# Block-sorted attention and a maxout layer in one kernel: W2 turned by DMA in place of TensorE, with the first two items' work in another order

## The chip, the cores and the metric

One NeuronCore of a Trainium2 chip runs the whole program. The metric is the device time of one execution in microseconds (us); a version's time is the median of its runs. A profiled execution gives the page and the trace that are read here.

## The reference

```python
# attention: q, k, v are [4, 8, 768, 64], sort_net is [4, 8, 8, 8]
P = sort_net
for _ in range(5):
    P = P - max(P, axis=-1);  P = exp(P)
    P = P / (sum(P, axis=-1) + 1e-09)
    P = P / (sum(P, axis=-2) + 1e-09)
k_sorted = einsum('bhij,bhjcd->bhicd', P, k_blocks)      # 8 blocks of 96 rows
v_sorted = einsum('bhij,bhjcd->bhicd', P, v_blocks)
attn = softmax(scale * q_block @ k_sorted_block.T)       # inside a block only
x = attn @ v_sorted_block                                # to [3072, 512]
# maxout layer: w1, w2 are [512, 1024], w_out is [1024, 512]
out = maximum(x @ w1, x @ w2) @ w_out                    # [3072, 512], float32
```

## The kernel before, in words

The kernel works on four batch items of 768 tokens. It uses max(h1, h2) = relu(h1 - h2) + h2. So it forms W1 - W2 once (`w_difference`, L229), takes relu(x(W1 - W2)) as `g` (`moe_h`, L685), and puts the h2 part into one small matrix, wc = W2 Wout (`w_product`, L654). The output is then g Wout + x wc, twelve matmuls in two halves of six for each 128 tokens (`out_products`, L700).

W2 is needed turned for `w_product`. `w2_transposes` (L634) does that on TensorE: 16 transposes of 128x128 into a PSUM tile, copied to `w2T` by ACT or DVE. It is called twice, by the steps `tw0D` and `tw1A`.

For an item the steps are these. Loads go out on POOL's queue and cast float32 to bf16 on the way (`load_q`, `load_k`, `load_v`, `load_w`, `load_w_columns`, L132 to L189). `sort_k` (L449) and `sort_v` (L473, L493, L516) multiply with a block-diagonal form of P; for v, `turn_v` (L242) first copies the raw item into another order. `q_transposes` (L413) is TensorE work for items 0 and 1 and a DMA transpose on SP for items 2 and 3, after `pair_q` (L403) on DVE. `scores` (SC, L539) is eight small matmuls and one exp on ACT (about 0.8 us); `values` (VA, L567) is eight small matmuls, a reciprocal and a product on DVE. `x_transposes` (TR or tx, L600) turns x to `xT`: on TensorE for item 0, by a DMA on SP for the others. An x tile holds two VA, and a transpose waits for both. SC unit u has head pair u % 4 and token half u // 4; TR t has half t // 2 and reads VA 2t and 2t + 1.

All PSUM tiles share four buffers (L62). Copies out of PSUM go to ACT or DVE: named by the caller, or picked by `pick` (L96), which keeps a running load of both engines with fixed costs in ns. TensorE, ACT, DVE, POOL and SP each run their instructions in program order (`manual_schedule`, L64), so the order of the Python calls is each engine's order.

The start is hand-ordered. TensorE streams zero columns (`keep_streaming`, L77) while ACT and DVE do the five rounds on P (`sinkhorn`, L264); `p_bf` is P at the end. L762 to L777 issue POOL's work: W1 and W2 by column pieces, Wout, two of four W differences, and item 1's k. The list `front` (L783) then gives item 0's steps in order: `k`, `v`, `tq`, `SC`, `VA`, `tx`, `tw`, `diff`, `pe` (masks of later items) and `hCTa`, `hCTb` (token half C, column group T of `moe_h`, in two parts), with a last letter A or D for the copying engine; `F` adds a fill of 512 columns to the next step. Ahead of its last 26 steps stand the loads of q(1), v(1), v(2), k(2) (L830).

After that, item b's MoE work runs as units (L909): eight `moe_h`, then twelve halves of `moe_out`; for item 0, eight empty ones, four `w_product` (units 8 to 11) and twelve halves (12 to 23). After unit n come the steps that a table (`first_tail`, `second_tail`, `third_tail`) lists under n: the next item's attention. Two tiles make one output store of 512 KB on SP, after units 15, 19 and 23. `load_q(2)` reuses W2's buffer, `load_q(3)` and `load_k(3)` reuse `v_raw`.

Of the kernel before, what the change touches and what calls it, by code (L numbers as in the profile page):

```python
# [11 lines left out]
BF16 = mybir.dt.bfloat16  # L12
# [4 lines left out]
def kernel(  # L17
# [16 lines left out]
    nc = tc.nc  # L34
# [4 lines left out]
    B, H, S, D = q.shape  # L39
    NB = sort_net.shape[-1]  # L40
    BLK = S // NB
    G = B * H
# [109 lines left out]
    def load_k(b):  # L152
        k_raw[b] = (
            kpool.tile([128, HB * D], BF16, tag="k_raw", name="k_raw")
            if b < 3
            else v_raw[:, 0 : HB * D]
        )
        n = HB * D // NCH
        for ci in range(NCH):
            nc.gpsimd.dma_start(  # L160
                out=k_raw[b][:, ci * n : (ci + 1) * n],
                in_=k_src[b, :, ci * n : (ci + 1) * n],
            )

    def load_v(b, pieces=2, which=None, half=None):
        r0 = (b % 2 if half is None else half) * 64
        n = BLK * D // pieces
        for m in range(pieces) if which is None else [which]:
            nc.gpsimd.dma_start(
                out=v_raw[r0 : r0 + 64, m * n : (m + 1) * n],  # L170
                in_=v_src[b, :, m * n : (m + 1) * n],
            )
# [5 lines left out]
    def load_w(dst, src):  # L178
        s = src.rearrange("(t p) f -> p t f", p=128)
        n = s.shape[1] // 2  # L180
        for i in range(2):
            nc.gpsimd.dma_start(
                out=dst[:, i * n : (i + 1) * n, :], in_=s[:, i * n : (i + 1) * n, :]
            )

    def load_w_columns(dst, src, t0, t1):
        s = src.rearrange("(t p) f -> p t f", p=128)
        c = slice(t0 * DFF // 4, t1 * DFF // 4)
        nc.gpsimd.dma_start(out=dst[:, :, c], in_=s[:, :, c])  # L189
# [13 lines left out]
    def selections(b, eng=nc.gpsimd):  # L203
        heads = {0: (0, 1), 2: (2, 1), 3: (3, 3)}.get(b)
        if heads:
            sel_v[b] = const.tile([G, 2, 8, NB], BF16, tag=f"sel_v{b}", name="sel_v")
            for half, item in enumerate(heads):
                eng.tensor_copy(
                    out=sel_v[b][:, half],
                    in_=ident[0:G, item * 8 : item * 8 + 8].to_broadcast([G, 8, NB]),  # L210
                )
        if b == 0:
            return
        sel_k[b] = const.tile([G, 8, 16], BF16, tag=f"sel_k{b}", name="sel_k")
        eng.tensor_copy(
            out=sel_k[b], in_=ident[0:G, b * 8 : b * 8 + 8].to_broadcast([G, 8, 16])
        )
# [11 lines left out]
    def w_difference(t, eng=None):  # L229
        n = DFF // 4  # L230
        (eng or nc.vector).tensor_tensor(
            out=w1_sb[:, :, t * n : (t + 1) * n],
            in0=w1_sb[:, :, t * n : (t + 1) * n],
            in1=w2_sb[:, :, t * n : (t + 1) * n],
            op=ALU.subtract,
        )
        if not eng:
            load["D"] += 600
# [392 lines left out]
    w2T = big.tile([128, NFB, DMODEL], BF16, tag="w2T", name="w2T")  # L631
    wc = big.tile([128, HP, DMODEL], BF16, tag="wc", name="wc")

    def w2_transposes(t, eng):  # L634
        ps = ps_bf16("tw_ps")
        for n in range(16):
            fb, dmt = t * 4 + n // 4, n % 4
            nc.tensor.matmul(  # L638
                ps[:, n * 128 : (n + 1) * 128],
                w2_sb[:, dmt, fb * 128 : (fb + 1) * 128],  # L640
                ident,
                is_transpose=True,
                start=True,
                stop=True,
            )
        return lambda: evac(
            w2T[:, t * 4 : t * 4 + 4, :].rearrange("p f d -> p (f d)"),
            ps,
            2048,
            two_x=True,  # L650
            eng=eng,
        )

    def w_product(dmt):  # L654
# [95 lines left out]
        return SC, VA, TR  # L750

    first, second, both = slice(0, 64), slice(64, 128), slice(0, 128)
    keep_streaming(ps_f32("fill_ps"), 86 * 126, most=126)
    for it in range(5):
        sinkhorn(it)
        if it < 3:
# [5 lines left out]
    for c, n, m in [(2, 2, 0), (4, 3, 1)]:  # L762
# [1 line left out]
            out=maskJ[:, c : c + n],  # L764
            in_=maskJ[:, m].to_broadcast([128, NB, n]).transpose([0, 2, 1]),
        )
    for t in range(2):
        load_w_columns(w2_sb, moe_w2, t, t + 1)
        load_w_columns(w1_sb, moe_w1, t, t + 1)
    for b in range(1, B):  # L770
        selections(b)
    load_w_columns(w2_sb, moe_w2, 2, 4)
    load_w_columns(w1_sb, moe_w1, 2, 4)
    load_w(wo_sb, moe_w_out)
    w_difference(0, nc.gpsimd)
    w_difference(1, nc.gpsimd)
    load_k(1)  # L777
    turn_v(first, "A", 36, 56)
    turn_v(first, "A", 56, 80)
    block_diagonals_first()  # L780
    turn_v(first, "D", 80, 96)

    front = """  # L783
        k0D k1A k2D v1D v2A v3A tq0D v0A tq1D SC1 SC0 F1
        SC2 VA1 SC5 VA0 SC3 F2 VA2 SC4 F0 tx0D SC6 VA3
        SC7 h00a VA4 tx1A tw0D h01a VA5 h01bA diff2 h00bA VA7 tx2A
        tw1A h02a VA6 h02bA h11a diff3 tx3A h12a h03a h12bD h10a h10bA
        pe2 h11bD h03bA h13a h13bA
    """.split()
    fills = [0]  # L790

    def fills_due():
# [3 lines left out]
    def front_step(step):  # L796

        eng = step[-1] if step[-1] in "AD" else None
        name = step[:-1] if eng else step
        kind = name.rstrip("0123456789ab")  # L800
        n = [int(x) for x in name if x.isdigit()]
        if kind == "F":
            fills[0] = 512
        elif kind == "k":
            sort_k(0, n[0], 640 if step == front[0] else 0, eng)
        elif kind == "v":
            sort_v(0, n[0], 0, eng)
        elif kind == "tq":
            q_transposes(0, n[0], eng)
        elif kind == "SC":  # L810
            scores(0, n[0], fills_due())
        elif kind == "VA":
            values(0, n[0], fills_due())
        elif kind == "tx":
            x_transposes(0, n[0], eng)
        elif kind == "tw":
            w2_transposes(n[0], eng)()
        elif kind == "diff":
            w_difference(n[0])
        elif kind == "pe":  # L820
            block_diagonals([(0, 2), (0, 3), (1, 1), (1, 2), (1, 3)], 2)
        elif name[-1] == "a":
            moe_h_products(0, n[0], n[1], (0, 2), fills_due())
        else:
            moe_h(0, n[0], n[1], eng, (1, 3))

    for step in front[:-26]:
        front_step(step)

    load_q(1)  # L830
# [14 lines left out]
    def sorts_and_scores(b):  # L845
# [5 lines left out]
    TQ = [lambda half=half: q_transposes(1, half) for half in range(2)]  # L851
    TURN = [lambda c=c: turn(both, c) for c in (0, 24, 48, 72)]
    first_tail = {
        7: KS,
        9: [TQ[0], TURN[0]],
        10: [SC[0], TQ[1], TURN[1]],
        11: SC[1:4] + TURN[2:4] + [lambda half=half: load_v(3, half=half) for half in range(2)],
        12: VS[0:3],
        13: VS[3:6],
        14: VS[6:8] + [SC[4]],  # L860
        15: [VA[0], lambda: pair_q(2, 0)],
        16: [VA[1], lambda: pair_q(2, 1)],
        17: SC[5:8] + [TR[0]],
        18: [VA[2]],
        19: [VA[3], TR[1]],
        20: [VA[4]],
        21: [VA[5], TR[2]],
        22: [VA[6], VA[7], TR[3]],
    }
    SC, VA, TR, KS = sorts_and_scores(2)  # L870
    VS = [lambda t=t: sort_v_halved(3, t) for t in range(4)]
    TURN = [lambda c=c: turn(both, c) for c in (0, 24, 48, 72)]
    second_tail = {
        0: [lambda: q_transposes(2, 0), lambda: q_transposes(2, 1)],
        2: KS,
        4: SC[0:2],
        5: [VA[0]],
        6: SC[2:4] + [TURN[0]],
        7: [VA[1], TR[0]],
        8: [VA[2], TURN[1]],  # L880
        9: [VA[3], TR[1], TURN[2]],
        10: SC[4:7],
        11: [VA[4], TURN[3]],
        12: [VA[5], TR[2], lambda: load_k(3), lambda: load_q(3)],
        13: [VA[6]],
        14: SC[7:8] + VS[0:2],
        15: [VA[7], TR[3]],
        16: VS[2:4],
        17: [lambda: pair_q(3, 0)],
        18: [lambda: pair_q(3, 1)],  # L890
    }
    SC, VA, TR, KS = sorts_and_scores(3)
# [69 lines left out]
```

The softmax here doesn't subtract the row's maximum and nothing guards it: scores larger than these inputs give would overflow.

## Time and profile before

| | |
|---|---|
| median of 3 runs | 166.72 us (166.19 to 168.2) |
| profiled execution, its own time | 166.46 us |
| its span, first to last instruction | 164.7 us |
| TensorE matmul busy | 159.5 us |
| ACT, DVE, POOL busy | 83.1, 76.4, 32.7 us |
| granted TensorE clock, mean | 0.999 |
| loads on POOL's queue (q0) | 13.37 MB |
| stores and transposes on SP's queue (q1) | 10.17 MB |

PE is TensorE, PEld its weight loads, SP the engine that issues stores and transposes. The page divides the span into 40 slices of 4.1 us and gives each engine's busy share in tenths. The chain of work that ended last follows the end back from one wait to what released it; each row is a start, a duration and the work. Timelines list an engine's instructions with start, duration, line, tiles and, in brackets, the idle time ahead and what ended it. A window row gives each engine's busy time in a stretch, the granted clock, the share of the DMA engines, and GB/s.

### The profile page before, as it was taken

To read this page: it belongs to the slowest core of one execution; us is meant where nothing else is said; L and a number is where in the kernel's file an instruction comes from. 1 tells how busy PE (TensorE), PEld (TensorE's weight loads), DVE (VectorE), ACT (ScalarE), POOL (GpSimd) and SP (SyncE) were. 2 spreads that over 40 slices of the span, in tenths; PEclk is the share of its full clock that TensorE was granted. 3 is DMA by queue.
4 is the path that set the end of the run, shared out by engine and by line. 5 is a ranking of instruction groups with operands and counts; after the bars stand their busy time and mean duration, and the time that the engine had idled before them with its cause. 6 is when DMAs were issued, how large, how long until landed. Compare 5 with 4: busy or idle time off the path is not lost.

```text
span 164.7 us, 4563 instructions
## 1 busy us (share of the span) xinstructions
PE 159.5 (97%) x2018; PEld 96.6 (59%) x2018; DVE 76.4 (46%) x169; ACT 83.1 (50%) x102; POOL 32.7 (20%) x59
## 2 busy tenths in 40 slices
PE   7999899999999999999999999999999999999992
PEld 7958678756554555557655554575655546554451
DVE  5869778556375564535277863250642320000011
ACT  3585995918139846055652262557447206642020
POOL 7989687150104000000014010000000000000000
PEclk9999999999999999999999999999999999999999
DMA  3999999999999995688425999991025293000333
GB/s 51 200 204 197 199 208 205 210 204 220 207 205 211 218 232 108 175 116 210 98 31 97 186 193 227 184 229 12 0 52 175 50 179 128 0 0 0 127 131 128
DMA packets 30404, 23.90 MB, mean 145 GB/s; under 512 B 16752, under 2 KB 25200, under 8 KB 30384
## 3 DMA queue, kind: packets, MB, share of 16 engines
q0 software_dynamic: 11040, 13.37, 48.4%
q1 hardware_dynamic: 19200, 10.17, 26.2%
q8 instruction: 16, 0.26, 0.6%
q10 hardware_dynamic: 144, 0.07, 0.1%
q14 instruction: 4, 0.03, 0.1%
HBM read 26.75 MB, written 6.29 MB: 201 GB/s over the span
## 4 chain that ended last, share of the span: by engine, by line
PE 93%; DVE 3%; ACT 1%; issue 1%
PE out_ps L704 38%; PE h_ps L677 26%; PE fill_ps L82 6%; PE o_ps L575 5%; PE wc_ps L657 4%; PE s_ps L548 4%; PE k_ps L458 3%; PE tq_ps L433 2%; DVE kT L110 1%; PE v_ps L523 1%; PE tw_ps L638 1%; ACT e L556 1%; PE tx_ps L613 1%; PE v_ps L500 1%; DVE qT L110 1%
## 5 line engine op out<-in xcount | busy, mean ns | idle before, releaser
L704 PE MATMUL out_ps<-wo_sb,g 128*128 128x512 bf16 (+2 forms) x200 | 48.3, 371 | 0.1
L677 PE MATMUL h_ps<-xT,w_sb 128*128 128x384 bf16 x256 | 44.5, 326 | 0.0
L677 PEld LDWEIGHTS <-w_sb 128*128 128x128 bf16 x256 | 24.0, 98 | 15.6
L556 ACT ACTIVATE e<-s_ps 96x768 bf16<-96x768 f32 x32 | 23.9, 804 | 13.6 <-PE s_ps L548 13.3
L691 ACT ACTIVATE g<-h_ps 128x768 bf16<-128x768 f32 x27 | 21.8, 811 | 17.4 <-PE h_ps L677 17.3
L704 PEld LDWEIGHTS <-g 128*128 128x128 bf16 x200 | 17.1, 97 | 15.8
L704 PE MATMUL out_ps<-wc,xT 128*128 128x512 bf16 (+2 forms) x100 | 24.8, 370 | 0.0
L108 ACT COPY o<-out_ps 128x1024 f32<-128x1024 f32 x10 | 10.1, 1012 | 28.0 <-PE out_ps L704 25.2
L592 DVE TENSOR_TENSOR x<-o_ps,rs 96x512 bf16<-96x512 f32 x32 | 22.0, 687 | 1.1
L704 PEld LDWEIGHTS <-xT 128*128 128x128 bf16 x100 | 9.6, 97 | 11.2
L575 PEld LDWEIGHTS <-e 96*128 96x128 bf16 x256 | 11.8, 97 | 5.9 <-DVE v_sb L110 0.2
L586 DVE RECIPROCAL rs<-o_ps 96x8 f32<-96x8 f32 x32 | 6.4, 201 | 17.7 <-PE o_ps L575 17.5
L739 DVE COPY o<-out_ps 128x512 f32<-128x512 f32 (+1 forms) x2 | 1.2, 625 | 27.6 <-PE out_ps L704 27.6
L575 PE MATMUL o_ps<-v_sb,e 96*128 96x65 bf16 x256 | 12.9, 193 | 0.0
L110 DVE CAST kT<-k_ps 128x1024 bf16<-128x1024 f32 x7 | 8.3, 1215 | 9.4 <-PE k_ps L458 9.4
L108 ACT CAST v_sb<-v_ps 96x1024 bf16<-96x1024 f32 x10 | 9.8, 1013 | 2.5 <-PE v_ps L479 0.9
L693 DVE TENSOR_SCALAR g<-h_ps 128x768 bf16<-128x768 f32 x5 | 4.8, 956 | 10.8 <-PE h_ps L677 10.8
L110 DVE CAST v_sb<-v_ps 96x1024 bf16<-96x1024 f32 x6 | 7.3, 1217 | 5.1 <-PE v_ps L523 2.2
L160 POOL DMA_DIRECT2D v_raw<-in_k_dram x3 | 2.5, 839 | 35.2 <-DVE v_dc L250 31.4
L548 PEld LDWEIGHTS <-kT 64*128 64x128 bf16 x256 | 6.1, 94 | 5.5 <-issue 3.6
L548 PE MATMUL s_ps<-qT,kT 64*128 64x96 bf16 x256 | 8.6, 204 | 0.7 <-PE o_ps L575 0.4
L82 PE MATMUL fill_ps<-fill 128*128 128x126 bf16 x86 | 7.8, 280 | 1.2 <-DVE fill L73 1.2
(95 smaller groups left out, 143.5 us busy)
## 6 DMA issues: line engine op xcount, KB each, us to landing
out_dram<-o SPq DMA_DIRECT2D x11, 512.0 KB, 3.1
v_raw<-in_v_dram POOLq DMA_DIRECT2D x8, 384.0 KB, 12.7
k_raw<-in_k_dram POOLq DMA_DIRECT2D x9, 256.0 KB, 9.9
w_sb<-in_moe_w_dram POOLq DMA_DIRECT2D x4, 256.0 KB, 9.2
w_sb<-in_moe_w_dram POOLq DMA_DIRECT2D x2, 512.0 KB, 10.6
wo_sb<-in_moe_w_out_dram POOLq DMA_DIRECT2D x2, 512.0 KB, 14.4
v_raw<-in_v_dram POOLq DMA_DIRECT2D x3, 256.0 KB, 4.6
q_raw<-in_q_dram POOLq DMA_DIRECT2D x4, 192.0 KB, 8.8
```

Source lines behind the costliest of these rows:

```text
L82: nc.tensor.matmul(ps[:, 0:w], w0, fill[:, 0:w], start=True, stop=True)
L108: nc.scalar.copy(out=out_ap, in_=in_ap)
L110: nc.vector.tensor_copy(out=out_ap, in_=in_ap)
L548: nc.tensor.matmul(ps[:, h2 * 512 + ii * 128 : h2 * 512 + ii * 128 + BLK], kT[b][rows, (hp * 8 + i) * BLK : (hp * 8 + i) * BLK + 128], rhs ...
L556: nc.scalar.activation(out=e[:, 0 : 8 * BLK].rearrange("p (t c r) -> p t c r", t=8, r=R), in_=ps[0:BLK] .rearrange("p (t f) -> p t f", t=8 ...
L575: nc.tensor.matmul(ps[:, h2 * 512 + ii * 65 : h2 * 512 + (ii + 1) * 65], e[:, (h2 * 4 + ii) * BLK : (h2 * 4 + ii) * BLK + 128], v_sb[:, m0 ...
L586: nc.vector.reciprocal(out=rs, in_=ov[:, :, :, 64])
L592: nc.vector.tensor_tensor(out=x, in0=ov[:, :, :, 0:D], in1=rs.to_broadcast([BLK, 2, 4, D]), op=ALU.mult,)
L657: nc.tensor.matmul(ps[:, 0:512], w2T[:, fb, dmt * 128 : (dmt + 1) * 128], wo_sb[:, fb, :], start=(fb == 0), stop=(fb == NFB - 1),)
L677: nc.tensor.matmul(h_ps[ch, t][:, m * 512 : m * 512 + TCH], w1_sb[:, hp, fb * 128 : (fb + 1) * 128], xT[:, b % 2, ch, hp % 2, hp // 2, :], ...
L691: nc.scalar.activation(out=g, in_=src, func=AF.Relu)
L704: nc.tensor.matmul(dst, g_tiles[b, ch, m // 2][:, m % 2, off : off + 128] if m < NFB else xT[:, b % 2, ch, hp % 2, hp // 2, off : off + 12 ...
```

## The change

W2 is turned by four DMA transposes on SP, one for each 128 rows, and `tw` and its PSUM tiles go. The loads of W are issued in another order and at other places: W2's first piece after `p_bf`, the others after the first sorted k. This is done by small POOL copies into a new tile `seen`, each of which reads a few elements of what is to be waited for. A third copy reads `w2T` at the third transpose and stands ahead of the loads of q(1), v(1), v(2) and k(2). Item 0's list has another order, token half 1 first, and four fills in place of three, which now add up. The opening fill is 92 matmuls of 118 columns in place of 86 of 126. Item 1's attention moves from units 7 to 22 to units 11 to 23, `pair_q(2)` moves into the second table, and most of item 2's steps move by one or two units.

```diff
-    def w2_transposes(t, eng):
-        ps = ps_bf16("tw_ps")
-        for n in range(16):
-            fb, dmt = t * 4 + n // 4, n % 4
-            nc.tensor.matmul(
...
+    def w2_transposes(dmt):
+        nc.sync.dma_start_transpose(
+            out=w2T[:, :, dmt * 128 : (dmt + 1) * 128],
+            in_=w2_sb[:, dmt, :],
         )
...
-    keep_streaming(ps_f32("fill_ps"), 86 * 126, most=126)
+    keep_streaming(ps_f32("fill_ps"), 92 * 118, most=118)
...
-    for t in range(2):
-        load_w_columns(w2_sb, moe_w2, t, t + 1)
-        load_w_columns(w1_sb, moe_w1, t, t + 1)
-    for b in range(1, B):
-        selections(b)
-    load_w_columns(w2_sb, moe_w2, 2, 4)
-    load_w_columns(w1_sb, moe_w1, 2, 4)
-    load_w(wo_sb, moe_w_out)
-    w_difference(0, nc.gpsimd)
-    w_difference(1, nc.gpsimd)
-    load_k(1)
     turn_v(first, "A", 36, 56)
     turn_v(first, "A", 56, 80)
     block_diagonals_first()
+    seen = const.tile([128, 3, 2], BF16, tag="seen", name="seen")
+    nc.gpsimd.tensor_copy(out=seen[0:G, 0], in_=p_bf[:, NB - 1, NB - 2 :])
+    load_w_columns(w2_sb, moe_w2, 0, 1)
+    selections(1)
+    selections(2)
     turn_v(first, "D", 80, 96)
 
     front = """
-        k0D k1A k2D v1D v2A v3A tq0D v0A tq1D SC1 SC0 F1
-        SC2 VA1 SC5 VA0 SC3 F2 VA2 SC4 F0 tx0D SC6 VA3
-        SC7 h00a VA4 tx1A tw0D h01a VA5 h01bA diff2 h00bA VA7 tx2A
-        tw1A h02a VA6 h02bA h11a diff3 tx3A h12a h03a h12bD h10a h10bA
-        pe2 h11bD h03bA h13a h13bA
+        k1A k0A v1D k2A v2A v0D tq0D v3A tq1D SC4 SC5 F2
+        F3 VA4 SC6 SC7 VA5 F0 SC0 VA6 SC1 VA7 F1 SC3
+        tx2D SC2 tx3D VA1 h10a VA0 VA2 h10bA h11a tx0A h11bA diff3
+        VA3 diff2 h13a h01a tx1D h03a h13bD h03bD h01bA h12a pe2 h00a
+        h02a h00bD h02bA h12bA
     """.split()
...
-            fills[0] = 512
+            fills[0] += 512
...
-    for step in front[:-26]:
+    front_step(front[0])
+    c0 = int(front[0][1]) * 16
+    nc.gpsimd.tensor_copy(out=seen[:, 1], in_=kT[0][:, c0 : c0 + 2])
+    load_w_columns(w1_sb, moe_w1, 0, 1)
+    load_w_columns(w2_sb, moe_w2, 1, 2)
+    selections(3)
+    load_w_columns(w1_sb, moe_w1, 1, 2)
+    load_w_columns(w1_sb, moe_w1, 2, 4)
+    load_w_columns(w2_sb, moe_w2, 2, 4)
+    load_w(wo_sb, moe_w_out)
+    for dmt in range(HP):
+        w2_transposes(dmt)
+    w_difference(0, nc.gpsimd)
+    w_difference(1, nc.gpsimd)
+    load_k(1)
+    nc.gpsimd.tensor_copy(out=seen[:, 2], in_=w2T[:, NFB - 1, 382:384])
+    for step in front[1:-26]:
         front_step(step)
...
     first_tail = {
-        7: KS,
-        9: [TQ[0], TURN[0]],
-        10: [SC[0], TQ[1], TURN[1]],
-        11: SC[1:4] + TURN[2:4] + [lambda half=half: load_v(3, half=half) for half in range(2)],
-        12: VS[0:3],
-        13: VS[3:6],
-        14: VS[6:8] + [SC[4]],
-        15: [VA[0], lambda: pair_q(2, 0)],
-        16: [VA[1], lambda: pair_q(2, 1)],
-        17: SC[5:8] + [TR[0]],
-        18: [VA[2]],
-        19: [VA[3], TR[1]],
-        20: [VA[4]],
-        21: [VA[5], TR[2]],
-        22: [VA[6], VA[7], TR[3]],
+        11: KS,
+        12: [TQ[0]],
+        13: [SC[0], TQ[1]],
+        14: SC[1:4] + TURN[0:2],
+        15: SC[4:5] + TURN[2:4] + [lambda half=half: load_v(3, half=half) for half in range(2)],
+        16: SC[5:8],
+        17: VS[0:3],
+        18: VS[3:6],
+        19: VS[6:8],
+        20: [VA[0], VA[1]],
+        21: [VA[2], VA[3], TR[0], TR[1]],
+        22: [VA[4], VA[5], TR[2]],
+        23: [VA[6], VA[7], TR[3]],
     }
...
     second_tail = {
-        0: [lambda: q_transposes(2, 0), lambda: q_transposes(2, 1)],
+        0: [lambda: pair_q(2, 0), lambda: pair_q(2, 1)],
+        1: [lambda: q_transposes(2, 0), lambda: q_transposes(2, 1)],
         2: KS,
-        4: SC[0:2],
-        5: [VA[0]],
-        6: SC[2:4] + [TURN[0]],
-        7: [VA[1], TR[0]],
...
+        5: SC[0:2],
+        6: [VA[0], TURN[0]],
+        7: SC[2:4],
+        8: [VA[1], TR[0], TURN[1]],
...
```

More of the change, by code (lines that the diff above doesn't have):

```diff
@@ L632 @@
     wc = big.tile([128, HP, DMODEL], BF16, tag="wc", name="wc")
-    def w2_transposes(t, eng):
-        ps = ps_bf16("tw_ps")
-        for n in range(16):
-            fb, dmt = t * 4 + n // 4, n % 4
[L638 to L651, printed above, removed]
+    def w2_transposes(dmt):
+        nc.sync.dma_start_transpose(
+            out=w2T[:, :, dmt * 128 : (dmt + 1) * 128],
+            in_=w2_sb[:, dmt, :],
         )
@@ L815, in front_step @@
             x_transposes(0, n[0], eng)
-        elif kind == "tw":
-            w2_transposes(n[0], eng)()
         elif kind == "diff":
@@ L873 @@
     second_tail = {
-        0: [lambda: q_transposes(2, 0), lambda: q_transposes(2, 1)],
+        0: [lambda: pair_q(2, 0), lambda: pair_q(2, 1)],
+        1: [lambda: q_transposes(2, 0), lambda: q_transposes(2, 1)],
         2: KS,
-        4: SC[0:2],
-        5: [VA[0]],
-        6: SC[2:4] + [TURN[0]],
-        7: [VA[1], TR[0]],
-        8: [VA[2], TURN[1]],
-        9: [VA[3], TR[1], TURN[2]],
+        5: SC[0:2],
+        6: [VA[0], TURN[0]],
+        7: SC[2:4],
+        8: [VA[1], TR[0], TURN[1]],
+        9: [VA[2], TURN[2]],
         10: SC[4:7],
-        11: [VA[4], TURN[3]],
-        12: [VA[5], TR[2], lambda: load_k(3), lambda: load_q(3)],
-        13: [VA[6]],
+        11: [VA[3], TR[1], TURN[3]],
+        12: [VA[4], lambda: load_k(3), lambda: load_q(3)],
+        13: [VA[5], TR[2]],
         14: SC[7:8] + VS[0:2],
-        15: [VA[7], TR[3]],
+        15: [VA[6]],
         16: VS[2:4],
-        17: [lambda: pair_q(3, 0)],
+        17: [VA[7], TR[3], lambda: pair_q(3, 0)],
         18: [lambda: pair_q(3, 1)],
```

## The prediction

> **What bounds the kernel now.** I read the page first, then the chain of work that ended last, then one-microsecond windows, the timelines of POOL, DVE and SP, and last the DMA queues in short windows.
>
> ```profile
> span 164.7 us, 4563 instructions
> PE 159.5 (97%) x2018; PEld 96.6 (59%) x2018; DVE 76.4 (46%) x169; ACT 83.1 (50%) x102; POOL 32.7 (20%) x59
> DMA  3999999999999995688425999991025293000333
> ```
>
> TensorE works in all but 5 us, of which 1.2 lie ahead of its first matmul and 3 behind its last. DMA is full from slice 1 to 14 (4 to 62 us). So TensorE sets the end, and the loads are close behind it in the first 62 us.
>
> ```profile
> 24.97 0.89 PE tw_ps L638 x16
> ...
> 28.68 0.89 PE tw_ps L638 x16
> ...
> 35.61 2.71 PE h_ps L677 x16
> 38.31 1.64 PE k_ps L458 x96
> 39.95 3.56 PE wc_ps L657 x16
> ```
>
> In the chain the W2 transposes are on the path (1.78 us). The first item ends at 38.31, where the second item's `sort_k` follows; the product that reads `w2T` starts at 39.95.
>
> ```profile
> 18.00:19.00 1.00, 0.84 (x21) 0.56 (x18) 0.88 (x1) 0.94 (x2) 0.00 (x0) 1.00 1.40 187
> 19.00:20.00 1.00, 0.70 (x16) 0.49 (x15) 0.21 (x2) 1.00 (x3) 0.78 (x1) 1.00 1.47 196
> 20.00:21.00 1.00, 0.75 (x22) 0.62 (x24) 0.77 (x3) 0.96 (x2) 1.00 (x1) 1.00 1.32 202
> ```
>
> The second figure of a row is TensorE's busy time in that microsecond, the last one the GB/s moved. From 14 to 21 us TensorE is idle for 0.84 us in all; from 21 us to its last matmul it lacks 0.13. With the 1.78 this makes 2.6 us, and apart from fills (0.2 each) the change cannot win more.
>
> **What the Trainium skill says.** "DMA: Bandwidth & Descriptors", section "Queues, rings and completion order": each DMA engine goes round-robin between queues, a packet at a time. The DMA windows from 98 to 100 us, where `load_q(3)` meets an xT transpose, agree:
>
> ```profile
> q0 software_dynamic: 405, 0.31, 101.2%
> q1 hardware_dynamic: 272, 0.07, 27.5%
> ```
>
> In the next 2 us it is 354 to 462, so about one packet for one (0.25 KB for a transpose, 0.77 for q, about 1 for W, 2 for k, 6 for v). From 90 to 92 it is 672 against 59: not always so. The same page, section "Latency and other measured facts", gives 261 GB/s for a transpose whose middle dimension is strided, as `w2T`'s is. Here xT and qT, whole at the destination, show about 200 (0.79 MB of qT in 3.9 us). "TensorE: Matmul & The Clock Gate", section "Back-to-back issue gap", gives N/2.4 + 2.5 ns: 56 ns for 128 columns, and 0.89/16 is 56.
>
> **The change part by part.**
>
> *Opening fills.* 92 x 118 = 10856 columns in place of 86 x 126 = 10836; by that price cold (N/1.2) and warm agree within 0.05 us, and 12 fills of 512 and the wait for `p_bf` follow anyway: 0.
>
> *W2's transposes.* Two groups of 0.89 go: -1.78. Their evacuations (1.23 us DVE, 1.87 ACT) were beside matmuls and win nothing by themselves.
>
> *First item in another order.* I stepped the new list through with durations of the trace: e 0.77 apart, VA 0.24 on TensorE and 0.85 apart on DVE, half an h group 0.65, tx 0.34 and 0.54 or 0.80 to evacuate. Sorts and q transposes give the same evacuations to ACT and DVE, so the first e starts at 18.4 as now. DVE then sets the pace: VA4 to VA7 end at 23.05, tx2 at 23.6, tx3 at 24.3, and h10a starts at 24.05, which puts the end of the list at 36.15. Against 38.31 that is -2.15: the 1.78 and 0.35 of idle time (one fill of 0.22 more is in it). An error of 0.5 either way is likely.
>
> *W loads later.*
>
> ```profile
> 9.46 2.34 POOL L189 DMA_DIRECT2D w_sb<-in_moe_w_dram  x3
> ...
> 19.22 2.12 POOL L231 TENSOR_TENSOR w_sb<-w_sb 128x1024 bf16<-128x1024 bf16 x1 [1.56 <-DMA w_sb<-in_moe_w_dram]
> ...
> 25.64 0.92 POOL L143 DMA_DIRECT2D q_raw<-in_q_dram  x1
> ```
>
> POOL's queue is served in order of issue at about 205 GB/s: v, k and q of item 0 (2.36 MB) end at 15.9 by the summed windows, then each 0.26 MB piece of W takes 1.3 us. That gives 18.5 for the second piece, and w_difference(0) starts at 19.2. After: w2's piece 0 is issued at 11.3, behind `p_bf`; `w1`'s piece 0 at 14.2, behind the first kT (ACT, 13.9). Both are ahead of 15.9, so the queue never runs dry: 0. Three pieces, selections(3) and wo take POOL until 20.1; w_difference(0) then ends at 22.2 and (1) at 24.35; h10a wants the first at 24.05, h11a the second at 25.85. The last W2 piece lands at 26.9; DVE's diff3 waits for it, with VA3's rescaling behind, and ends at 27.6; h13a can start at 27.75. The cover here is 0.15 us: a microsecond of delay in W2 is a microsecond on the path.
>
> *Four DMA transposes.* SP has nothing else until 55 us. They start at 26.95, 1024 packets each, about 1.4 us of issue each (xT 1.22 for 768). At 28.1 the load queue still holds some 460 packets of wo and 384 of k. If served one for one, 844 of 4096 packets have gone when k ends at 35.3, and the rest follow alone. At 200 GB/s (0.83 MB, 4.2 us) the four land near 36, 37.4, 38.7 and 40. w_product wants them at 36.2, 38.0, 39.8 and 41.6: 0 to 0.2, taken as 0. If they win over the loads (the other ratio) all land by 34. k of item 1 slips from 35.7 to 36 to 38.7; its sort now comes at 43.5.
>
> *The gate on POOL.* Behind `seen[2]` stand load_q(1), four v pieces and load_k(2), then load_q(2). They are issued at 33 to 39 in place of 25.64, but before they were only queued: q(1) ended at 38.9. Now it lands at 43 to 45, and TQ0 wants it at 46.4. The v pieces (3.85 us for two) land by 48.5 and 52.7; TURN wants them at 50.6 and 52.3: 0 to 0.4 on DVE, taken as 0. v(3) ends at 65 to 68 in place of 61.3.
>
> *Second item later.* The same TensorE work is squeezed from 16 units into 12. Two waits appear. (a) VS6 and VS7 now come in unit 19, with its output evacuation ahead of them on DVE or ACT; VA0 one unit (1.30) later needs all of v_sb. VS7's copy ends about 1.85 after its matmuls, so 0.55 of wait; e5 to e7 on ACT hold up VS2's PSUM buffer by another 0.2 to 0.4, which I bound at 0 to 1.0 and take with (a) as 0.55. (b) TR1, now in unit 21:
>
> ```profile
> 69.52 0.20 DVE L586 RECIPROCAL rs<-o_ps 96x8 f32<-96x8 f32 x1 [0.62 <-PE o_ps L575]
> 69.76 0.69 DVE L592 TENSOR_TENSOR x<-o_ps,rs 96x512 bf16<-96x512 f32 x1
> 70.37 0.20 DVE L586 RECIPROCAL rs<-o_ps 96x8 f32<-96x8 f32 x1
> 70.59 0.69 DVE L592 TENSOR_TENSOR x<-o_ps,rs 96x512 bf16<-96x512 f32 x1
> ```
>
> These two VA started on TensorE at 69.08, and the second x is ready 2.2 later. TR1 then lands 2.8 to 3.7 later (8.3 under loads): 5.05 at least from the start of VA2. TensorE has 2 x 1.30 + 3 x 0.49 = 4.07 until item 1's h, and 0.33 to the matmul that reads TR1: a wait of 0.65 at least, 1.55 at 3.7, up to 3 if v(3)'s last packets share the engines. I take 0.65. TR3 stands behind a 512 KB store on SP, but its reader comes 7 us on: 0.
>
> *Second tail.* pair_q(2) moves behind h; its transposes (5.6) land ahead of SC in unit 5 (10.5 us on). The rest moves one or two units with slack: 0.
>
> Sum: -2.15 + 0.55 + 0.65 = -0.95, which makes a span of 163.75 against 164.7. Outside the span lie 1.8 us (166.46 - 164.7), untouched; on the median of 166.72 it gives 165.8.
>
> **Rivals.** (1) *Nothing is given back:* both waits vanish because ACT and DVE place their copies better than I stepped. 166.72 - 2.15 = 164.6. For it: before, the same VS copies made no gap. Against: TR1's 5.05 exceeds 4.4.
> (2) *The packed attention becomes the bound:* 1.0 for PSUM, 3 for TR1 under v(3), 0.4 for late v, 0.5 of the front's gain lost: 166.72 - 1.65 + 4.4 = 169.5; about half of it is 167.5. For it: an xT transpose took 8.3 us beside loads.
> (3) *Slower: the W2 transposes starve.* They keep less than their rate, by the strided destination or by loads. What remains at 35.3 is 0.83 MB, and the fourth is wanted at 41.6, so below 130 GB/s TensorE waits, and below about 115 the gain is gone. At 75 GB/s it lands at 46.4: +4.8, and 165.8 + 4.8 = 170.6. For it: an xT transpose under k loads ran at some 100 GB/s. Against: the gate keeps new loads out.
> (4) *It isn't what it says:* no, w_product reads only what the DMA wrote.
>
> **How the numbers follow.** Chances: forecast 0.50 (own range 164.9 to 166.8), rival 1 0.18, rival 2 0.20, rival 3 0.12. Two per cent, about what a measurement of this kernel can tell from no change, is 163.4 and 170.1. Below 163.4 exceeds the 2.6 us ceiling: 0.03, for scatter of the runs. Above 170.1: 0.10 of rival 3's 0.12 and 0.04 of rival 2's 0.20: 0.14. Within: 0.83. Range 164.0 to 169.3, which leaves out the worst of rival 3 and the tail of rival 2.
>
> **What would show it.** No tw_ps rows; the last h matmul of item 0 ends near 36 (over 37 refutes the stepping). wc_ps follows without a gap, or rival 3 holds. POOL's q_raw load starts between 33 and 39. Item 1's h has a gap of 0.6 to 1.6 at its third matmul. A wait of DVE or PE for a w_sb, q_raw or v_raw load ahead of 60 us would break the "0" of the load steps.

## The result and the profile after

The changed kernel takes 172.26 us (171.5 to 174.1) against 166.58 for the kernel before on the same chip: a ratio of 1.031, with an interval of 1.021 to 1.040. The forecast was 165.8 with a range of 164.0 to 169.3, so the change is slower where "about the same" was forecast. The profiled execution took 171.9 us. Of two runs below, e9 and e11, only the times and one figure of the clock are used, since e9's profiled execution ran at half clock from 21.4 to 28.3 us and e11's at 0.95 throughout.

First the page, the same three rows that were read of the kernel before:

```profile
span 169.8 us, 4501 instructions
PE 157.6 (93%) x1974; PEld 94.1 (55%) x1993; DVE 75.7 (45%) x169; ACT 80.4 (47%) x100; POOL 33.6 (20%) x62
DMA  3999999997999999999104999986025353000333
```

TensorE's matmuls sum to less (157.6 against 159.5 us; of the 1.9, a part is 19 matmul records that this trace lacks, x1974 beside x1993 weight loads) in a span that is 5.1 us longer: most of the loss is waiting. The DMA row used to be full to 62 us. Now (a digit is 4.2 us) it has a dent in its tenth digit, from 38 to 42 us, and is full again up to 80. The loads end later. The chain that ended last says where it hurts:

```profile
27.19 10.61 DMA w2T<-w_sb
...
44.93 1.64 PE k_ps L458 x96
...
67.73 6.55 DMA xT<-x
74.42 5.33 PE h_ps L663 x24
79.75 1.64 PE k_ps L458 x96
```

Two DMA transposes are now links of the chain, where the chain before had TensorE's `tw_ps`. The second `k_ps` row (the third item's sort) is a good mark, because the same work stands ahead of it in both kernels, `tw` and the fills aside. The chain before has

```profile
71.02 3.90 PE h_ps L677 x24
74.92 1.63 PE k_ps L458 x96
```

so the mark was at 74.92 and is now at 79.75, 4.83 later. From there to TensorE's end nothing more is lost (161.65 and 166.51: 4.86). So the whole answer lies ahead of 80 us. TensorE's timeline there, with the idle time and what ended it in brackets:

```profile
37.85 7.08 PE L643 MATMUL wc_ps<-wo_sb,w2T 128*128 128x512 bf16 x31 [1.23 <-DMA w2T<-w_sb]
...
65.48 0.66 PE L575 MATMUL o_ps<-v_sb,e 96*128 96x65 bf16 x16 [0.47 <-DVE v_sb L110]
...
74.42 5.33 PE L663 MATMUL h_ps<-xT,w_sb 128*128 128x384 bf16 x24 [2.91 <-DMA xT<-x]
```

Three waits, and one thing that is no wait: 24 h matmuls took 5.33 us, where the chain before has 3.90 for the same 24. The windows (second figure TensorE's busy time, then weight loads, DVE, ACT, POOL, the granted clock, DMA share, GB/s) show why:

```profile
72.00:73.00 1.00, 0.00 (x0) 0.00 (x0) 0.97 (x4) 0.06 (x1) 0.00 (x0) 1.00 1.58 144
73.00:74.00 1.00, 0.00 (x0) 0.00 (x0) 0.99 (x3) 0.00 (x0) 0.00 (x0) 0.81 0.98 198
...
76.00:77.00 1.00, 1.00 (x5) 0.50 (x4) 0.00 (x0) 0.00 (x0) 0.00 (x0) 0.50 1.00 268
```

While TensorE waited, its clock fell to half, and it stayed there until 77.0. The wait of 2.91 so cost another 1.43.

**Why the xT transpose was late.** POOL's timeline around the gate, and its last loads of v(3):

```profile
39.64 0.19 POOL L821 COPY seen<-w2T 128x2 bf16<-128x2 bf16 x1 [13.83 <-DMA w2T<-w_sb]
39.88 0.90 POOL L143 DMA_DIRECT2D q_raw<-in_q_dram  x1
...
53.99 0.53 POOL L169 DMA_DIRECT2D v_raw<-in_v_dram  x1 [5.52 <-DVE v_dc L250]
57.64 1.56 POOL L169 DMA_DIRECT2D v_raw<-in_v_dram  x3 [3.13 <-DVE v_dc L250]
```

POOL stood 13.8 us at the copy that reads `w2T`. All loads behind it, q(1) first, were issued from 39.88 on. The load queue (q0) had run dry before that, while SP's queue (q1) worked on: DMA windows (queue, packets, MB, share) from 37 to 38 us, then from 66 to 68 us:

```profile
q1 hardware_dynamic: 1009, 0.25, 128.5%
```

```profile
q0 software_dynamic: 83, 0.41, 100.3%
q1 hardware_dynamic: 7, 0.01, 2.1%
```

From 36 on the engines carried almost nothing but W2's transposes, and from 40 to 42 almost nothing (21 GB/s in each microsecond) until the first new load got going. That is some 6 us almost without loads at a time when they are the scarce thing: about four in which the transposes had the engines to themselves, and two in which nothing did. The debt shows at 66 to 68: v(3) still holds the engines in packets of 5 KB on average. The 7 packets of SP's queue are not transposes yet. They have 2 KB each and belong to an output store that was issued at 64.33, ahead of item 1's transposes, and that took until 73.5 to land. The first two transposes were issued at 67.73 and 69.52, their first packet of 256 bytes moved at 71.6, when v(3)'s packets were nearly over, and they landed 6.5 and 5.5 us after their issue.

### The profile page after: what moved, and what is told of

The parts are those of the page before. It is cut to its first block, busy times and chain, and to the rows that moved or that the text cites. A ratio compares the mean times of both kernels' runs of the same rounds, so it can differ in the third digit from the quotient of the medians.

```text
span 169.8 us, 4501 instructions
## 1 busy us (share of the span) xinstructions
PE 157.6 (93%) x1974; PEld 94.1 (55%) x1993; DVE 75.7 (45%) x169; ACT 80.4 (47%) x100; POOL 33.6 (20%) x62
## 4 chain that ended last, share of the span: by engine, by line
PE 68%; DMA 17%; DVE 5%; ACT 3%; issue 2%; POOL 2%; SPq 0%; ACTq 0%
PE out_ps L690 33%; PE h_ps L663 19%; DMA w2T<-w_sb 6%; DMA w_sb<-in_moe_w_dram 6%; PE wc_ps L643 4%; DMA xT<-x 4%; PE k_ps L458 3%; PE o_ps L575 3%; PE s_ps L548 3%; POOL w_sb L189 2%; ACT e L556 1%; DMA p_sb<-in_sort_net_dram 1%; PE v_ps L523 1%; PE tq_ps L433 1%; DVE colsum L276 1%
## 5 line engine op out<-in xcount | busy, mean ns | idle before, releaser
L663 PE MATMUL h_ps<-xT,w_sb 128*128 128x384 bf16 x256 | 45.4, 332 | 3.0 <-DMA xT<-x 2.9
L690 PE MATMUL out_ps<-wo_sb,g 128*128 128x512 bf16 (+2 forms) x185 | 45.8, 370 | 1.5 <-issue 1.1
L663 PEld LDWEIGHTS <-w_sb 128*128 128x128 bf16 x256 | 24.5, 99 | 19.5 <-DVE q_pair L407 3.0
L556 ACT ACTIVATE e<-s_ps 96x768 bf16<-96x768 f32 x32 | 23.8, 808 | 13.8 <-PE s_ps L548 13.6
L108 ACT COPY o<-out_ps 128x1024 f32<-128x1024 f32 x9 | 9.1, 1013 | 28.2 <-PE out_ps L690 25.6
L110 DVE CAST kT<-k_ps 128x1024 bf16<-128x1024 f32 x5 | 5.9, 1221 | 19.5 <-PE k_ps L458 19.5
L575 PEld LDWEIGHTS <-e 96*128 96x128 bf16 x256 | 10.9, 97 | 6.4 <-DVE v_sb L110 1.0
L575 PE MATMUL o_ps<-v_sb,e 96*128 96x65 bf16 x256 | 12.3, 193 | 0.9 <-DVE v_sb L110 0.5
L110 DVE CAST v_sb<-v_ps 96x1024 bf16<-96x1024 f32 x7 | 8.5, 1219 | 5.5 <-PE v_ps L523 2.6
L108 ACT CAST v_sb<-v_ps 96x1024 bf16<-96x1024 f32 x9 | 8.9, 1008 | 2.2 <-PE v_ps L500 0.9
L643 PE MATMUL wc_ps<-wo_sb,w2T 128*128 128x512 bf16 x31 | 7.0, 379 | 1.3 <-DMA w2T<-w_sb 1.2
```

The lines of the kernel that those rows point to most:

```text
L556: nc.scalar.activation(out=e[:, 0 : 8 * BLK].rearrange("p (t c r) -> p t c r", t=8, r=R), in_=ps[0:BLK] .rearrange("p (t f) -> p t f", t=8 ...
L575: nc.tensor.matmul(ps[:, h2 * 512 + ii * 65 : h2 * 512 + (ii + 1) * 65], e[:, (h2 * 4 + ii) * BLK : (h2 * 4 + ii) * BLK + 128], v_sb[:, m0 ...
L643: nc.tensor.matmul(ps[:, 0:512], w2T[:, fb, dmt * 128 : (dmt + 1) * 128], wo_sb[:, fb, :], start=(fb == 0), stop=(fb == NFB - 1),)
L663: nc.tensor.matmul(h_ps[ch, t][:, m * 512 : m * 512 + TCH], w1_sb[:, hp, fb * 128 : (fb + 1) * 128], xT[:, b % 2, ch, hp % 2, hp // 2, :], ...
L690: nc.tensor.matmul(dst, g_tiles[b, ch, m // 2][:, m % 2, off : off + 128] if m < NFB else xT[:, b % 2, ch, hp % 2, hp // 2, off : off + 12 ...
```

## The experiments

Theory A: the turning of W2 by DMA is the loss, through the order in which the DMA engines then serve things. Its transposes have to share with the loads, the gate then holds all later loads, so v(3) runs into item 1's transposes, and the clock falls behind that gap. Rival B: the packed second item (and the new order) are the loss in themselves, by ACT, DVE and PSUM. Rival C: the gate's wait is the loss, and without it all would be well.

| run | what differs | us | ratio to before (interval) |
|---|---|---|---|
| changed kernel | | 172.26 | 1.031 (1.021 to 1.040) |
| e1 | changed, no gate | 189.9 | 1.133 (1.128 to 1.138) |
| e2 | changed, TensorE turns W2 | 170.94 | 1.025 (1.020 to 1.030) |
| e3 | changed, half of v(3) | 169.78 | 1.019 (1.016 to 1.022) |
| e4 | changed, fills ahead of item 1's h | 171.58 | 1.028 (1.024 to 1.033) |
| e5 | before, new tables only | 169.1 | 1.015 (1.013 to 1.017) |
| e6 | changed, gate earlier | 173.16 | 1.033 (1.028 to 1.037) |
| e7 | changed, v(3) later | 175.26 | 1.054 (1.048 to 1.060) |
| e8 | e6 and e7 and spread VA | 176.61 | 1.063 (1.057 to 1.070) |
| e9 | before, new order only | 168.37 | 1.010 (1.008 to 1.012) |
| e10 | changed, old tables | 174.83 | 1.051 (1.046 to 1.055) |
| e11 | changed, nothing turned | 166.82 | 1.001 (0.999 to 1.003) |
| e12 | e9, nothing turned | 165.94 | 0.995 (0.993 to 0.997) |

**e1, no gate.**

```diff
-    nc.gpsimd.tensor_copy(out=seen[:, 2], in_=w2T[:, NFB - 1, 382:384])
```

> The changed kernel without the third POOL copy, so that the loads of q(1), v(1), v(2) and k(2) no longer wait for w2T. Theory A (the cost is the order in which the DMA engines serve loads and transposes): the w2T transposes now stand beside q and v packets too, so w2T lands after 43 instead of 37.8 to 40.7, the wait of TensorE at w_product grows from 1.65 us to over 5, the v(3) loads end earlier and the wait at item 1's first h shrinks; in all 171 to 176 us. Rival C (the 3 us in which the gate leaves the DMA engines idle are the loss): the time falls to 167 to 169. Rival B (the packing of item 1's attention into units 11 to 23): within 1 us of 172.3.

TensorE's timeline, and SP's with the four transposes in one row:

```profile
60.53 3.65 PE L643 MATMUL wc_ps<-wo_sb,w2T 128*128 128x512 bf16 x9 [17.61 <-DMA w2T<-w_sb]
```

```profile
28.50 31.12 SPq L635 DMA_TRANSPOSE w2T<-w_sb  x4
```

With the loads let through, the four transposes take 31 us and the product waits 3.08 and 17.61. So rival C falls: without the gate the loss is far larger. This is the forecast's third rival (the transposes starve), with more than four times the wait it was given there (4.8). The wait and the time were also far larger than Theory A had on record. The DMA windows, from 36 to 40 us and from 44 to 48, show how the two queues share:

```profile
q0 software_dynamic: 695, 0.56, 91.9%
q1 hardware_dynamic: 689, 0.17, 37.4%
```

```profile
q0 software_dynamic: 149, 0.72, 93.1%
q1 hardware_dynamic: 147, 0.04, 8.3%
```

It is one packet for one. But a transpose's packet has 256 bytes, and v's have 6 KB: beside them the transposes moved 0.04 MB in 4 us.

**e2, TensorE turns W2, all else as changed.**

```diff
-        VA3 diff2 h13a h01a tx1D h03a h13bD h03bD h01bA h12a pe2 h00a
+        VA3 diff2 h13a h01a tw0A tx1D h03a tw1A h13bD h03bD h01bA h12a pe2 h00a
...
-    for dmt in range(HP):
-        w2_transposes(dmt)
...
-    nc.gpsimd.tensor_copy(out=seen[:, 2], in_=w2T[:, NFB - 1, 382:384])
```

> The changed kernel with W2 turned on TensorE again (two groups of 16, after h01a and h03a), without the DMA transposes and without the gate on w2T; order of item 0, W loads and tails as changed. Theory A: no wait at w_product, v(3) ends near 63 us, ahead of TR0 and TR1, so that the wait at item 1's first h is 0.6 to 1.5 us and the clock stays up: 166.5 to 168.5. Rival B: the gap at item 1's first h stays near 2.9 us with the clock falling behind it: 170 or more.

The late xT transpose is gone as Theory A has it: the wait at item 1's h is 0.58 and the clock holds. The time missed the expectation by 2.4. TensorE's timeline shows where, around the place where `tw` was put back:

```profile
31.73 0.81 PE L677 MATMUL h_ps<-xT,w_sb 128*128 128x384 bf16 x4 [0.65 <-DVE xT L110]
32.69 1.05 PE L638 MATMUL tw_ps<-ident,w_sb 128*128 128x128 bf16 x16 [0.15 <-ACT w2T L108]
```

Item 0 ends at 39.95 there, 3.3 later than in the changed kernel: 1.78 is `tw`, the rest is mostly waits (the two shown, and one of 0.62 for a W difference, ending at 28.37). That the new order has no room for the two copies of `w2T` on ACT is likely, but only the wait of 0.15 names one. e2 is therefore no clean measure of "the change without its DMA transposes"; e11 was made for that.

**e3, half of v(3).**

```diff
-        15: SC[4:5] + TURN[2:4] + [lambda half=half: load_v(3, half=half) for half in range(2)],
+        15: SC[4:5] + TURN[2:4] + [lambda: load_v(3, half=1)],
```

> The changed kernel with v(3) loaded once, to one half of the partitions, instead of twice (left out: half of the reads for item 3's v, which then uses old data there), so that the loads end 3.9 us earlier. Theory A: TR0 and TR1 no longer stand behind 6 KB packets; the gap at item 1's first h falls from 2.9 to 0.6 to 1.5 us, the clock doesn't fall, 168 to 169.5. Rival B: no change of the gap, 171 to 172.5.

```profile
73.32 3.73 PE L663 MATMUL h_ps<-xT,w_sb 128*128 128x384 bf16 x22 [0.71 <-DMA xT<-x]
```

The gap at item 1's h goes from 2.91 to 0.71, the clock holds, and from the end of the product for wc to the mark it takes 31.35 us in place of 34.82. The time falls by some 2 us (ratio 1.019 in place of 1.031), a little less than expected (in this execution the product ended 0.8 later). So it is v(3)'s packets that hold up the output store and item 1's transposes behind it.

**e4, TensorE kept busy through the gap.**

```diff
-        units = [lambda ch=ch, t=t: moe_h(b, ch, t) for ch in range(2) for t in range(4)]
+        units = [
+            lambda ch=ch, t=t: moe_h(b, ch, t, n=6656 if (b, ch, t) == (1, 0, 0) else 0)
+            for ch in range(2)
+            for t in range(4)
+        ]
```

> The changed kernel with 13 fills of 512 columns (2.8 us of TensorE) ahead of item 1's first h, where TensorE waits. If the granted clock of 0.50 behind the gap costs the 1.43 us by which the 24 h matmuls are longer (5.33 against 3.90), the time falls by 1.2 to 1.5 us, to about 171, with the gap for xT still there. If the clock falls for another reason (a clock that changes by itself), the time stays within 0.5 us of 172.3 or grows by the fills.

```profile
75.76 3.74 PE L663 MATMUL h_ps<-xT,w_sb 128*128 128x384 bf16 x22 [0.22 <-DMA xT<-x]
```

22 h matmuls take 3.74 us here: full clock. From the product's end to the mark it takes 33.66, 1.16 less. The clock term is real in the trace; the two times' intervals overlap, so the total alone would not show it.

**e5, only the new tables, on the kernel before.** The two tables `first_tail` and `second_tail` are those of the changed kernel.

> The kernel before with only the two tables of the changed one (item 1's attention in units 11 to 23, pair_q(2) and item 2 later); W2 stays on TensorE, loads and item 0's order as before. Theory A with the packing as a smaller term: v(3) ends near 63 us, ahead of TR0, so only the packing is paid: 0.4 us of longer output groups behind small matmuls, 0.5 of wait for v_sb, 0.6 for TR1: 168 to 169. Rival B (the packing is the main loss): 170.5 or more, with a gap of over 2 us at item 1's first h. If the packing costs nothing: 166.2 to 167.2.

```profile
72.58 3.73 PE L677 MATMUL h_ps<-xT,w_sb 128*128 128x384 bf16 x22 [0.52 <-DMA xT<-x]
```

The mark moves from 74.92 to 76.32: 1.40, of which 0.47 is the wait for `v_sb`, 0.52 this one, and the remaining 0.4 is in output groups that stand behind small matmuls. (The time is 2.6 longer: TensorE ends 1.73 later than before, and what follows its last matmul takes 3.96 us in place of 3.05, which no run explains.) The gap at item 1's h is close to the forecast's 0.65, not 2.9. The reason is in the DMA window from 66 to 68 us:

```profile
q1 hardware_dynamic: 250, 0.47, 62.0%
q0 software_dynamic: 25, 0.10, 23.9%
```

v(3) was issued at 54.28, no earlier than in the changed kernel (53.99), but by 66 all but some 25 of its packets had moved here: it landed at 69.2, and at 73.1 there. From 62 to 64 us e5's load queue moves 0.35 MB in 72 packets (4.9 KB on average, v's), the changed kernel's 0.39 MB in 283 (1.4 KB, the last of q(2)'s and the first of v's): there k(2) and q(2) had stood in front of v(3) until then. Rival B is thus a real term of its own, but a smaller one; the larger gap needs the late loads.

**e6, the gate earlier.** The transposes and the gate go ahead of the loads of Wout and k(1).

```diff
-    load_w_columns(w1_sb, moe_w1, 2, 4)
     load_w_columns(w2_sb, moe_w2, 2, 4)
-    load_w(wo_sb, moe_w_out)
+    load_w_columns(w1_sb, moe_w1, 2, 4)
...
-    load_k(1)
     nc.gpsimd.tensor_copy(out=seen[:, 2], in_=w2T[:, NFB - 1, 382:384])
+    load_w(wo_sb, moe_w_out)
+    load_k(1)
```

> The changed kernel with the gate on w2T put ahead of the loads of W_out and k(1) (and w2's last piece loaded ahead of w1's). Theory A: behind W the load queue is empty, so the four transposes run alone from about 26.5 us and land by 31 (10.1 to 10.6 us of landing for the first two become 3 to 5); w_product then waits for W_out, which lands at 37 to 38, by 0.5 to 1.5 us; v(3) ends 2 to 3 us earlier than in the changed kernel and the gap at item 1's first h shrinks: 168.5 to 171. If transposes are slow by themselves (the strided destination), they land after 34 in spite of the empty queue and the time stays at 172 or more.

```profile
25.15 6.54 SPq L635 DMA_TRANSPOSE w2T<-w_sb  x4
```

```profile
41.40 8.95 PE L643 MATMUL wc_ps<-wo_sb,w2T 128*128 128x512 bf16 x28 [2.01 <-DMA wo_sb<-in_moe_w_out_dram]
```

Now the transposes run nearly alone (6.54 us of issue in place of 11.62) and the gate opens at 32.4. But Wout is late in their place: the product waits 1.42 and 2.01 for it, and after the second wait its matmuls take 0.32 on average in place of 0.22, the slow clock again. v(3) landed no earlier (73.6), and the time missed the expectation. The time that the turning takes from the loads (W's last piece landed at 27.4, the next load was issued at 32.7) is only handed to another load.

**e7, v(3) after item 2's q transposes**, by a POOL copy that reads `qT` ahead of `load_v(3)`; `TURN` of item 3 moves to units 11 to 13.

> The changed kernel with the loads of v(3) behind a POOL copy that reads qT of item 2, so that TR0 to TR3 of item 1 and the qT transposes have the DMA engines without loads; item 3's turns move to units 11 to 13 of the second table. Theory A: TR1 lands 2.8 to 3.7 us after its issue, the gap at item 1's first h is 0.6 to 0.8 us, the clock stays up: 168.3 to 169.8, if the late v(3) costs nothing further on. Rival B: the gap stays, 171 or more.

The gap at item 1's h is 0.50 and the mark is at 76.64, 3.1 better, as Theory A has it. But `qT` landed only at 82.8, so v(3) (issued 83.8 in place of 54), k(3) and q(3) all came late, and TensorE pays further on, once for `v_dc` (1.92) and once for the last item's k:

```profile
119.50 4.28 PE L663 MATMUL h_ps<-xT,w_sb 128*128 128x384 bf16 x16 [4.70 <-DVE kT L110]
```

**e8**, e6 and e7 together, with the values of item 1 spread over one unit more and the gate on the second transpose.

> Early gate (one transpose earlier), v(3) behind qT as in the run before, and item 1's values spread over units 19 to 23 with VA2, VA3, TR0 and TR1 in unit 20 and SC5 to SC7 in unit 19. Theory A: the waits at w_product (but for W_out, 0 to 1.5), at v_sb and at item 1's first h go; what is left of the change is the 1.7 us that item 0 gains, less 0.4 for output groups behind small matmuls: 164.8 to 167. If something further is behind the loss: 168 or more.

A miss. No wait is left at the product or at item 1's h, but TensorE waits 1.90 for a W difference, 1.68 and 1.92 for `v_dc`, and 1.91 for item 3's kT. Loads that are moved out of one place are missing at another (but the wait for a W difference is there in other runs too, up to 1.50 in e10).

**e10, the old tables in the changed kernel.**

> The changed kernel with the two tables of the kernel before (item 1's attention from unit 7 on). Theory A: q(1), issued behind the gate at 39.6 us, lands near 47 us, but its transposes now stand two units earlier, ahead of two of the four w_product groups, so that TensorE waits about 3 to 5 us for q(1) and again for v; TR0 and TR1 then stand behind v(3) too; 172 to 176. If the packing is what costs most: 169 to 170.5.

```profile
49.59 1.49 PE L433 MATMUL tq_ps<-ident,q_raw 128*64 128x128 bf16 x24 [6.35 <-DMA q_raw<-in_q_dram]
```

With the second item where it was, TensorE waits 6.35 for q(1), which the gate holds; the expectation had 3 to 5. So the later place of item 1's attention belongs to the gate: the turning by DMA needs it, and e5's 1.40 is part of the turning's price.

**e9, only item 0's order and the adding fills, on the kernel before** (`tw` stays on TensorE: `tw0A` behind `tx0A`, `tw1A` behind `diff2`).

> The kernel before with only item 0's list of the changed one (and its adding fills), W2 turned on TensorE after tx0 and after diff2; loads of W, tables and opening fill as before. The prediction gave the order itself 0.35 us of gain beside the 1.78 of the transposes: 166.0 to 166.4 by it. If the order gains nothing, or the two copies of w2T on ACT hold it up: 166.4 to 167.5. Above 168 the order would be a cause of the loss of its own.

**e11, the changed kernel with nothing turned; e12, e9 with nothing turned.** Both compute wc from other values:

```diff
-                w2T[:, fb, dmt * 128 : (dmt + 1) * 128],
+                w1_sb[:, dmt, fb * 128 : (fb + 1) * 128],
```

> The changed kernel, but W2 is not turned at all: the four DMA transposes and POOL's copy that waits for them are gone, and the product for wc reads the W difference in place of the turned W2, so that its values are others. All else stays: order of item 0, W loads, packed second item. It shows what the change is worth with the turning free. Theory A (the loss is what the transposes and their gate do to the loads and to item 1's transposes): item 0's h ends near 36.6 as in the changed kernel, no wait at the product, 0.5 to 0.7 at item 1's h, clock kept; of the changed kernel's 79.75 for the sort that follows item 1's h, 1.65 + 2.3 + 1.43 go: 74.4 to 75.2, and 166.5 to 168 us in all. Rival (the packing and the order are the loss): 169 to 171. The sum on record (front -2.15, packing +1.2) would give 165.8.

> The kernel before with item 0's new order and its adding fills, and W2 not turned at all (no TensorE transposes, no copies of them; the product for wc reads the W difference, so that its values are others). Loads, opening fills and second item are those of before. If the new order alone is worth the forecast's -2.15 once the 1.78 of TensorE transposes are gone: item 0's h ends near 36.2 and the time is 164.4 to 165. If the order costs by itself what the run with TensorE transposes and the new order suggested (1.6 us): 166.2 to 166.8.

e11 decides between A and B: with order, W loads and packed tables all kept, and only the four transposes and their gate gone, the time is that of the kernel before (1.001). The turning and its gate are worth some 5 us (1.031 against 1.001). All the rest together comes to nothing, although TensorE's 1.78 of transposes are gone in e11 too: the order, the W loads and the packing use them up. (The wait at the product, put at 1.65 in that expectation, is the 1.23 of the timeline above.)

e9 lost 1.7 where the forecast had a small gain for the order. e12, whose time lies between its two expectations, shows that TensorE's turning is dear in the new order (168.37 - 165.94 = 2.4 for 1.78 of matmuls; 3.3 in e2). Its chain of work that ended last, at the end of item 0:

```profile
33.64 3.36 PE h_ps L656 x20
36.99 1.64 PE k_ps L458 x96
```

Item 0 ends at 36.99 in place of 38.31. A gain of 1.32 with all of the 1.78 of `tw` gone means that the order itself costs about 0.5 with the old loads. And of the 1.32 little arrives: TensorE then waits 0.61 for the exp of a score at 50.4 and 0.61 for `qT` at 79.0, and item 2's h starts at 103.83 against 104.03. In time it is 0.8 (166.7 - 165.94). How the order's cost divides over its steps was not tried.

Of the versions that turn W2 none beats the kernel before.

## Why the prediction was wrong, point by point

The terms at the mark (third item's sort, 74.92 before and 79.75 after), each measured:

| term | forecast | measured | from |
|---|---|---|---|
| end of item 0 | -2.15 | -1.69 | 38.31 and 36.62 |
| wait for `w2T` | 0 | 1.23 | TensorE's timeline |
| packing, with 0.5 at item 1's h | 1.2 | 1.40 | e5's mark |
| more of the wait at item 1's h | 0 | 2.39 | 2.91 - 0.52 |
| half clock behind it | not foreseen | 1.43 | 5.33 - 3.90 |
| sum | -0.95 | 4.76 | 4.83 seen |

*Opening fills, evacuations, first item in another order.* Right in kind: it ended 0.47 later than stepped (36.15), within the error given. That is in part luck: with the same work up to there it ended at 37.04 in e3, 37.81 in e4, 37.67 in e7 and 38.05 in e10, beyond the 37 that was to refute the stepping. e12 says that what was won is `tw`, and that the 0.35 of idle time was not.

*W loads later.* 0 came out in this execution (TensorE waited 0.08 for diff3), and the warning that the cover is thin was right: the same loads and the same list have a wait of 0.27 at that place in e3, 0.65 in e7, 0.94 in e4 and 1.50 in e10.

*Four DMA transposes, "0 to 0.2, taken as 0".* Wrong in size, but not in its rule. The step took one packet for one while loads are queued. The Trainium skill, "DMA: Bandwidth & Descriptors", section "Queues, rings and completion order", says that engines go round-robin between queues, a packet at a time, and the trace's packets agree. From 32 to 34 us they are

```profile
q0 software_dynamic: 199, 0.36, 95.0%
q1 hardware_dynamic: 196, 0.05, 18.1%
```

and e1 has 695 to 689. What was wrong is the start. The step counted from 28.1; the first transpose was issued at 27.19, and no packet of it moved before 31.1, 3.9 us later. It is 3.9 to 4.0 in e1, e3, e4, e7 and e10 too, and 1.3 in e6 and e8, where the load queue was about to end. Why it is so long beside queued loads, no run shows. So at 35.3 some 420 packets had gone, not 844. What was left then ran alone at 252 GB/s in the window shown and 284 in the next, near the 261 that the same page gives in "Latency and other measured facts" and above the 200 taken. The four landed at 37.8, 38.7, 39.6 and 40.7 where 36, 37.4, 38.7 and 40 were stepped: the late start put the first 1.8 late, and the first is the one that the product waits for.

*The gate on POOL, "taken as 0".* This is the step that failed. The time of issue was forecast closely (33 to 39, seen 39.88), and q(1) was in time for TensorE, though 2 us later than given (46.95). But "before they were only queued" was taken to mean that holding them costs nothing. That holds while the queue in front stays full. Here it ran dry at 36.6, the next load packet moved at 41.5, and some 6 us of loading were lost. So v(1) and v(2) came late (DVE waited 2.07 for `v_raw`, which the forecast had named as a sign against it), k(2) and q(2) stood in front of v(3), and v(3) landed at 73.1, where 65 to 68 was given. At the mark this is 2.39 + 1.43 = 3.82 of the 5.8 us between forecast and measured; 1.23 is the wait for `w2T`. e11 takes the turning and its gate away together, so how the loss divides between the gate and the transposes' own time on the DMA engines stays open.

*TR1, 0.65, "up to 3 if v(3)'s last packets share the engines".* The small size is right (0.52 in e5). The condition for the large one was named and its price was right (2.91), but it was put into rival 2 with a chance of 0.20, though it followed from the gate's step. Two steps were costed one by one, each with the other at its best. The transpose that h waited for is also TR0 (74.28) and not TR1. A 512 KB store stands ahead of both on SP's queue, which the step had for TR3 alone; whether the gap closes when that store is issued behind them was not tried.

*The clock.* No step had it. The Trainium skill, "TensorE: Matmul & The Clock Gate", section "Part 1: The HAM clock gate (the "warmup" mystery)", says that TensorE falls to half clock after an idle window of about 3.4 us, and needs about as long busy to come back. Here the mean of 0.81 from 73 to 74 puts the fall at 73.6, 2.1 after the last matmul (71.5), and full clock returns at 77.0, 2.6 after work resumed. The half clock so lasted 3.41 us, as long as the page's window, but 2.1 of idle time was enough to bring it on; there the measurement decides. The other traces narrow it down. Ahead of the last matmul, half clock lasts 3.41 us in all of them (e7, and twice in e8) or a multiple of it (6.83 in e6 and e10, 17.07 in e1). Counted from its changes in such steps, the clock fell after a step with 1.90 or 1.92 us idle (e8), 2.12 (the changed kernel) or 2.19 (e6), or idle throughout (e1, e7, e10); it held after steps with 1.67 and 1.68 (e8) or 1.85 (e1). The edge is near 1.9 us and not sharp, as e9's execution at reduced clock fell after 1.81. So e8's wait of 1.90, inside one step, cost the clock, and e7's of 1.92 and e1's of 3.08, each across two, did not. The wait of 2.91 had to be priced with the clock at risk.

*Rivals.* Rival 2 (169.5) had the mechanism, and lacked the clock and the wait for `w2T`. Rival 3 (170.6) had the direction and is what e1 shows, but in the changed kernel the gate turned that loss into late loads. Its "against", that the gate keeps new loads out, was true and was the cost.

*Ceiling.* No run won more than the 2.6 us; e12 shows that with the turning free some 0.8 of it arrives.

## What to carry to other kernels

A gate that holds loads back is free only as long as the DMA engines have other loads to carry: count the microseconds in which the load queue is empty behind it, and follow that debt to the last load and to whatever shares the engines with it. Work moved from a full TensorE to full DMA engines has not become cheaper, and here 1.78 us of matmuls became some 6 us almost without loads. A queue with small packets gets few bytes beside one with large packets, when they share packet for packet. And a wait of some 2 us or more on TensorE has to be priced with the slow clock that may follow it.

## What the runs showed of the hardware that was not expected

- Beside queued loads the DMA transposes got one packet for one (196 to 199 in the changed kernel, 689 to 695 and 147 to 149 in e1). With 256 bytes against v's 6 KB that is little: in e1 the four took 31 us of issue, against 6.5 when they ran nearly alone (e6).
- The first packet of the first W2 transpose moved 3.9 us after its issue in the changed kernel, where loads were queued, and 1.3 us after it in e6, where they were about to end. For item 1's first xT transpose it was 3.9 us beside v(3), and 1.2 in e7 without it.
- The clock fell after 2.1 us without matmuls, and 2.6 us of work at half clock followed. Thirteen fills of 512 zero columns in the gap (e4) kept it at full speed.
- Ahead of the last matmul, half clock lasts 3.41 us or a multiple of it in every trace that has it, and what brought it on was some 1.9 us or more of idle time inside one such step (1.90 in e8 did, 1.85 in e1 did not).
- The issue of a DMA transpose holds its engine: SP needed 11.62 us for four in the changed kernel and 6.54 in e6.
